# Linear attention and an eight-expert MoE on one Trainium2 core: token rows stored in 32 bits, split after the gather

## The chip, the core and the metric

The kernel runs on one core of one Trainium2 chip, in one launch. The metric is the device time of one execution in microseconds (us); lower is better. The times shown are the median of runs of the whole kernel, and the profile is of one execution.

Names of engines as in the profile: PE is TensorE's matmul, PEld its weight load, DVE is VectorE, ACT is ScalarE, POOL is GpSimd, SP is SyncE, which here only issues DMAs.

## The reference

Attention over 8 batches, 8 heads, 576 tokens and 64 columns per head with 128 random features, and then a mixture of 8 experts of which each token goes to one:

```python
q_s, k_s = q * scale, k * scale
def phi(x):
    h = einsum('bhsd,md->bhsm', x, omega) - sum(x * x, -1) / 2
    return exp(h - max(h, -1)) / sqrt(m)
kv = einsum('bhsm,bhsd->bhmd', phi(k_s), v);  z = sum(phi(k_s), axis=2)
attn = einsum('bhsm,bhmd->bhsd', phi(q_s), kv) / (einsum('bhsm,bhm->bhs', phi(q_s), z) + 1e-6)

x = attn as rows of tokens: [4608, 512]
logits = x @ w_gate;  e = argmax(logits);  gate = softmax(logits)[e]
eom = sigmoid(x @ w_output_gate)
out = gate * eom[e] * (relu(x @ w1[e]) @ w2[e])      # w1: 512 x 1024, w2: 1024 x 512
```

## The kernel before, in words

**Two halves, interleaved.** The attention is done in 32 units u, one for each head (8) and pair of batches (4 pairs j, 1152 tokens each, as 9 chunks of 128). When the eight units of a pair j are done, its tokens are routed. The experts' work is done in items of 128 rows that share an expert: list 0 has 8 items, list 1 has 8, list 2 has 9, and the last list has 24 places, of which 13 are used in the profiled execution, 38 items in all. Units of later pairs and items of earlier lists run at the same time; the last list's items run alone.

**Precision.** Matmul operands are split into two 16-bit halves, high (a cast) and low (the 32-bit value less the high half). The casts are on ACT or DVE, the subtractions mostly on POOL.

**A unit** (`unit`, line 453). After the matmuls `pn` with the values and with the gates' weights folded in, `divide` (719) scales the result on DVE into `xf(u)`: 9 chunks of 64 columns of the head's output and, beside them, 16 columns with this head's part of the logits. Then

- `hi_half` (742, instruction on line 743, DVE) casts the 64 columns to 16 bits into the tile `xs` of the head pair;
- `lo_half` (745, line 747, POOL) writes the low half beside it;
- `sum_up` (760, lines 763 to 767, POOL, the last one on DVE) adds the 16 logit columns to the sum `lga` over heads;
- `pair` (780, line 786, SP) writes `xs` of two heads to the DRAM tile `rows`, 512 bytes per token and head pair. A row of `rows` is 512 words of halves and 16 words of which the first is the token's scale.

**Routing** (`routing`, `listing`) is a chain of small DVE instructions that ends in the indices `gi` of the items' rows.

**An item** (`item`, 1369). `gather` (line 1446, POOL) fetches 128 rows by an indirect DMA into `gx(n)`, three buffers. Line 1458 (SP) turns the halves straight out of `gx(n)` by a transposing DMA into `xt(n)`, three buffers. `hidden` (line 1483, PE) multiplies them by w1, `relu` (1490, ACT) and `rest` (1494, DVE) make the two halves `hh` and `hl` of the hidden layer, `second` (1506 and 1514, PE) multiplies by w2, `scaled` (1567, ACT) scales by the word from `gx(n)` into `os(n)`, and `put` (1556, POOL) scatters the rows to the output. `gx(n)` comes free with `scaled(n)`, so gather n+3 waits for it. When the expert changes, new weights come by DMA (`bring`, lines 1402 and 1404, SP) and are split on ACT (`high`, 364) and DVE (`low`, 368).

**What sets the order.** Every step is given to `Plan` with its engine, an assumed cost, what it comes after and a rank. `Plan.order` (181) simulates the engines with these costs and writes one list; each engine executes its part of it strictly in that order. A step whose input is late holds up all that stands behind it on its engine. A gather is assumed to have landed 0.65 + 0.75 + 0.95 us after its instruction (at the earliest), and a change in any step's cost or inputs can move steps on all engines.

Of the kernel before, what the change touches and what calls it, by code (L numbers as in the profile page):

```python
# [21 lines left out]
P = 128  # L22
B, H, S, D, M = 8, 8, 576, 64, 128
NE, F = 8, 1024
N = B * S
DM = H * D
NSC = 4
NC = 9
NCV = 10
NP = H // 2  # L30
ROW = DM + 16
KEY = 64
KC = DM // P
GW = 2 * NE
W = 1 + D + GW
# [229 lines left out]
def attention_moe(ctx: ExitStack, tc: tile.TileContext, kqt, kqn, v, om, wg, w1, w2, cf, cm, ci, out):  # L265
    nc = tc.nc
# [34 lines left out]
    scales = const.tile([P, NC, ROW - DM], F32, name="scales")  # L301
# [108 lines left out]
    xf = buf("xf", 2, [NC, D + GW], F32)  # L410
    den = buf("den", 2, [NC], F32)
    xs = buf("xs", 2, [NC, P], F32)
# [40 lines left out]
    def unit(u):  # L453
        j, h = divmod(u, H)
# [262 lines left out]
        pr, o = u // 2, (u % 2) * D  # L717
# [13 lines left out]
        for c0, c1, pe, dve in ((0, 5, 0.6, 0.48), (5, NC, 0.42, 0.4)):  # L731
            plan.add(
                ("pn", u, c0), ("PE",), pe, lambda c0=c0, c1=c1: attend(c0, c1), after=[*turned_all, ("gl", u)], rank=R + 5,
                tiles=[("et", u), ("kvs", u)], bank=(cls, ("pn", u, c0), [c1 - c0, W]),
            )
            plan.chain(
                ("xf", u, c0), ("DVE",), (0.07, 0.1, dve), lambda c0=c0, c1=c1: divide(c0, c1), after=[("pn", u, c0)], rank=R + 5,
                tiles=[("xf", u), ("den", u)], frees=[("pn", u, c0)],
            )


        def hi_half():
            nc.vector.tensor_copy(xs(pr).bitcast(F16)[:, :, o : o + D], xf(u)[:, :, 0:D])  # L743

        def lo_half():
            x = xs(pr).bitcast(F16)
            nc.gpsimd.tensor_tensor(  # L747
                out=x[:, :, P + o : P + o + D], in0=xf(u)[:, :, 0:D], in1=x[:, :, o : o + D], op=ALU.subtract
            )

        plan.add(
            ("xh", u), ("DVE",), 0.37, hi_half, after=[("xf", u, 0), ("xf", u, 5)], rank=R + 6,
            tiles=[("xf", u), ("xs", pr)],
        )
        plan.add(
            ("xl", u), ("POOL",), 1.23, lo_half, after=[("xh", u)], rank=R + 6, tiles=[("xf", u), ("xs", pr)]
        )


        def sum_up():  # L760
# [12 lines left out]
            tiles=[("xf", u), ("lga", j)], bank=("e", ("rt", j), [512]) if end else None,  # L773
# [110 lines left out]
    def save_scales(j):  # L884
        nc.sync.dma_start(rows[j * NC * P : (j + 1) * NC * P, DM:].rearrange("(c p) r -> p c r", p=P), scales)
# [392 lines left out]

    gx = buf("gx", 3, [ROW], F32)
    xt = buf("xt", 3, [2 * KC, P], F16)  # L1280
# [88 lines left out]
    def item(n):  # L1369
# [75 lines left out]
        def gather():  # L1445
# [10 lines left out]
        )  # L1456
        add(
            ("xt", n), "SP", 0.63, lambda: nc.sync.dma_start_transpose(xt(n), gx(n)[:, 0:DM].bitcast(F16)),
            after=[("gx", n)], rank=-700.0 + n, tiles=[("xt", n), ("gx", n)], dma=0.9, turn=True,
# [105 lines left out]
        def scaled(w_):  # L1565
            d = DM * w_ // P
            nc.scalar.activation(os(n)[:, 0:d], banks["po", n][:, 0:d], AF.Copy, scale=gx(n)[:, DM : DM + 1])  # L1567
# [90 lines left out]
```

## Time and profile before

| | |
|---|---|
| runs | 667.91, 660.49, 665.92 us; median 665.92 |
| the profiled execution | 664.8 us, of which the span from the first to the last instruction is 663.0 |
| mean granted TensorE clock | 0.961 |
| busy: PE, DVE, ACT, POOL | 610.9, 425.7, 413.0, 340.5 us |
| DMA | 129.09 MB |
| first and last gather (line 1446) | 116.8 and 623.0 us |
| last unit's cast (line 743) | 465.4 us |

In order of time: 0 to 80 us are units in 32-bit matmuls, 80 to 130 the first routing, 130 to 440 units and items together, 440 to 500 the last routing beside items, and from 500 on items alone. Idle time of an engine costs something only where TensorE waits for it. In the views of waits a row reads: engine and line that waited, what it waited for, us in total, times, longest. In the timeline a row is start, duration, engine, line, operation, and in brackets idle time just before it.

### The profile page before, as it was taken

Reading aid. Unit: us, or ns where it says so; the run is one execution under the profiler, and the core shown is the slowest. Engines: PE = TensorE matmul, PEld = TensorE weight load, DVE = VectorE, ACT = ScalarE, POOL = GpSimd, SP = SyncE. Lnnn points to the kernel's source line nnn. Section 1 sums busy time; section 2 is a strip of 40 time slices with the busy share of each in tenths; the row PEclk is TensorE's granted clock in tenths of the full one; section 3 lists DMA queues with packets and bytes.
Section 4 is the critical chain, followed back from the end, with each engine's and each line's share of the span. In section 5 each row is a group of like instructions: output and inputs, shape, how many; then the busy total and the mean of one; then the engine's idle time right before and its main releaser. Section 6 shows DMA issues by size and latency. Waiting matters only on the chain. (4 is left out here: it accounts for less than half of the span.)

```text
span 663.0 us, 22360 instructions
## 1 busy us (share of the span) xinstructions
PE 610.9 (92%) x8732; PEld 479.8 (72%) x8732; DVE 425.7 (64%) x1277; ACT 413.0 (62%) x970; POOL 340.5 (51%) x235
## 2 busy tenths in 40 slices
PE   6999987799999899999788999999999899999972
PEld 6899976677777677777555777878677767676761
DVE  4899889876978897576587776753882611431160
ACT  5876887589989759898575588762611611521150
POOL 1342445569957958989376588965031312131110
PEclk9999977699999999999899999999999999999996
DMA  9544578997999979999999675877747647642730
GB/s 317 207 136 129 174 281 197 254 252 167 319 275 287 272 191 221 227 225 235 277 257 170 149 194 126 144 134 198 226 113 211 183 92 234 172 90 62 268 112 8
DMA packets 145895, 129.09 MB, mean 195 GB/s; under 512 B 104271, under 2 KB 127441, under 8 KB 144465
## 3 DMA queue, kind: packets, MB, share of 16 engines
q1 hardware_dynamic: 139760, 107.45, 64.0%
q0 software_dynamic: 5984, 19.72, 9.4%
q8 instruction: 85, 1.39, 0.9%
q14 instruction: 66, 0.53, 0.3%
HBM read 83.86 MB, written 19.30 MB: 156 GB/s over the span
## 5 line engine op out<-in xcount | busy, mean ns | idle before, releaser
L1483 PE MATMUL ph<-xt,w1h 128*128 128x128 f16 (+1 forms) x2432 | 205.2, 218 | 3.4 <-ACT os L1567 1.6
L1483 PE MATMUL ph<-xt,w1l 128*128 128x128 f16 (+1 forms) x1216 | 201.3, 218 | 0.0
L1483 PEld LDWEIGHTS <-w1h 128*128 128x128 f16 x2432 | 181.9, 98 | 10.8 <-issue 4.4
L543 ACT ACTIVATE ef<-pp,nb 128x128 f32<-128x128 f32 x576 | 162.8, 392 | 41.5 <-DVE nb L537 31.6
L1494 DVE SCALAR_TENSOR_TENSOR hl<-ph,hh 128x512 f16<-128x512 f32 (+1 forms) x76 | 50.6, 666 | 116.4 <-ACTq L1412 76.6
L566 POOL TENSOR_TENSOR es<-ef,es 128x1152 f16<-128x1152 f32 x44 | 104.9, 2391 | 35.6 <-ACT es L564 19.5
L524 DVE TENSOR_REDUCE pp<-pp 128x3 f32<-128x384 f32 x192 | 102.8, 557 | 28.2 <-PE pp L502 27.7
L1483 PEld LDWEIGHTS <-w1l 128*128 128x128 f16 x1216 | 118.5, 98 | 0.3 <-DVEq L1407 0.2
L1446 POOL DMA_INDIRECT gx<-rows,gi x38 | 40.8, 1074 | 140.5 <-ACT os L1567 100.6
L1514 PE MATMUL po<-w2h,hl 128*128 128x512 f16 x280 | 107.0, 382 | 2.4 <-DVEq L1412 1.5
L1514 PE MATMUL po<-w2h,hh 128*128 128x512 f16 x280 | 107.4, 384 | 0.0
L1514 PE MATMUL po<-w2l,hh 128*128 128x512 f16 x280 | 107.1, 383 | 0.0
L1490 ACT ACTIVATE hh<-ph 128x512 f16<-128x512 f32 (+1 forms) x76 | 44.3, 583 | 80.0 <-PE ph L1483 73.6
L1514 PEld LDWEIGHTS <-hh 128*128 128x128 f16 x560 | 51.9, 99 | 58.0 <-issue 3.7
L1567 ACT ACTIVATE os<-po,gx 128x512 f32<-128x512 f32 (+1 forms) x38 | 25.5, 670 | 72.9 <-PE po L1514 68.0
L436 POOL TENSOR_TENSOR xlo<-xt,xhi 128x1152 f16<-128x1152 f32 x24 | 57.2, 2382 | 13.2 <-ACT xhi L429 12.7
L713 PE MATMUL pn<-kvs,et 128*128 128x81 f16 (+1 forms) x960 | 48.2, 210 | 12.3 <-DMA et<-es 7.2
L713 PEld LDWEIGHTS <-et 128*128 128x128 f16 (+1 forms) x960 | 41.6, 105 | 21.2 <-DMA et<-es 7.9
L564 ACT CAST es<-ef 128x1152 f16<-128x1152 f32 x44 | 51.3, 1176 | 7.4 <-DMA et<-es 6.9
L1514 PEld LDWEIGHTS <-hl 128*128 128x128 f16 x280 | 27.6, 99 | 35.3 <-DVE hl L1494 1.3
L502 PE MATMUL pp<-omh,xhi 64*128 64x128 f16 x432 | 43.0, 223 | 5.0 <-DVE xf L726 2.7
L747 POOL TENSOR_TENSOR xs<-xf,xs 128x576 f16<-128x576 f32 x32 | 42.1, 1317 | 8.9 <-DVE xs L743 8.1
(183 smaller groups left out, 1052.8 us busy)
## 6 DMA issues: line engine op xcount, KB each, us to landing
r<-w SPq DMA_DIRECT2D x10, 2048.0 KB, 11.9
xt<-kqt SPq DMA_DIRECT2D x32, 576.0 KB, 4.7
xn<-kqn SPq DMA_DIRECT2D x24, 576.0 KB, 4.9
rawv<-v SPq DMA_DIRECT2D x32, 325.0 KB, 3.7
rows<-xs SPq DMA_DIRECT2D x16, 576.0 KB, 5.3
r<-w SPq DMA_DIRECT2D x8, 512.0 KB, 6.6
ef<-w SPq DMA_DIRECT2D x2, 512.0 KB, 4.4
et<-w SPq DMA_DIRECT2D x2, 512.0 KB
```

The lines of the kernel that those rows point to most:

```text
L436: lambda t0=t0, t1=t1: nc.gpsimd.tensor_tensor(out=xl(u)[:, t0:t1], in0=xt32(u)[:, t0:t1], in1=xh(u)[:, t0:t1], op=ALU.subtract),
L502: nc.tensor.matmul(banks["pp", 2 * u + i, g][:, c, :], x[r, t], w[r, :], start=(a == 0), stop=(a == len(ops) - 1))
L524: nc.vector.tensor_reduce(out=pp[:, 3, 0:3], in_=pp[:, 0:3, :], op=ALU.min, axis=AX.X)
L543: nc.scalar.activation(ef(n)[:, c, :], banks["pp", n, g][:, c % 3, :], AF.Exp, bias=nb(n)[:, c : c + 1], scale=-SK)
L564: nc.scalar.copy(es(slot_es(n))[:, 0], ef(n))
L566: nc.gpsimd.tensor_tensor(out=es(slot_es(n))[:, 1], in0=ef(n), in1=es(slot_es(n))[:, 0], op=ALU.subtract)
L713: nc.tensor.matmul(pn[lo:hi, c - c0, :], a[:, c, lo:hi], w[:, b, :], start=(i == 0), stop=(i == len(ops) - 1))
L747: nc.gpsimd.tensor_tensor(out=x[:, :, P + o : P + o + D], in0=xf(u)[:, :, 0:D], in1=x[:, :, o : o + D], op=ALU.subtract)
L1483: nc.tensor.matmul(ph[:, f4, 0:w_], w[qd][:, kk, fo : fo + P], xt(n)[:, x, 0:w_], start=(a == 0), stop=(a == 3 * KC - 1))
L1490: nc.scalar.activation(hh(n)[:, sl, 0:w_], banks["ph", n, g][:, :, 0:w_], AF.Relu)
L1494: nc.vector.scalar_tensor_tensor(out=hl(n)[:, sl, 0:w_], in0=banks["ph", n, g][:, :, 0:w_], scalar=0.0, in1=hh(n)[:, sl, 0:w_], op0=ALU.ma ...
L1514: nc.tensor.matmul(po, x(n)[:, f, :], w[f // 2][:, f % 2, :], start=(f == 0 and a == 0), stop=(f == FC - 1 and a == 2))
```

## The change

The 64 columns and the 16 logit columns stay together in 32 bits. `divide` writes straight into the pair's tile `xs`, now 9 x 2 x 80 words; `hi_half` and `lo_half` leave the unit, and `xf(u)` becomes a view of `xs`. The rows go to DRAM as they are, logits included: 320 bytes per token and head, so 640 in place of 512 per head pair, and a row of `rows` has 656 words in place of 528. Each item then splits its own 128 gathered rows: a cast on DVE (`row_half(0)`, step `xh`) and a subtraction on POOL (`row_half(1)`, step `xl`) from `gx(n)` into a new tile `xg(n)`, two buffers, and the transposing DMA reads `xg(n)`.

```diff
-ROW = DM + 16
+DW = D + GW
+XW = H * DW
+ROW = XW + 16
...
-    xf = buf("xf", 2, [NC, D + GW], F32)
     den = buf("den", 2, [NC], F32)
-    xs = buf("xs", 2, [NC, P], F32)
+    xs = buf("xs", 2, [NC, 2, DW], F32)
...
-        pr, o = u // 2, (u % 2) * D
+        pr = u // 2
+        xf = lambda u: xs(u // 2)[:, :, u % 2]
...
-                tiles=[("xf", u), ("den", u)], frees=[("pn", u, c0)],
-            )
-        def hi_half():
-            nc.vector.tensor_copy(xs(pr).bitcast(F16)[:, :, o : o + D], xf(u)[:, :, 0:D])
-        def lo_half():
-            x = xs(pr).bitcast(F16)
-            nc.gpsimd.tensor_tensor(
-                out=x[:, :, P + o : P + o + D], in0=xf(u)[:, :, 0:D], in1=x[:, :, o : o + D], op=ALU.subtract
-            )
-        plan.add(
-            ("xh", u), ("DVE",), 0.37, hi_half, after=[("xf", u, 0), ("xf", u, 5)], rank=R + 6,
-            tiles=[("xf", u), ("xs", pr)],
-        )
-        plan.add(
-            ("xl", u), ("POOL",), 1.23, lo_half, after=[("xh", u)], rank=R + 6, tiles=[("xf", u), ("xs", pr)]
-        )
+                tiles=[("xs", pr), ("den", u)], frees=[("pn", u, c0)],
+            )
...
-        both = [("xl", 2 * pr), ("xl", 2 * pr + 1)]
+        both = [("xf", 2 * pr + i, c0) for i in range(2) for c0 in (0, 5)]
...
-                rows[j * NC * P : (j + 1) * NC * P, hp * P : (hp + 1) * P].rearrange("(c p) r -> p c r", p=P), xs(pr)
+                rows[j * NC * P : (j + 1) * NC * P, hp * 2 * DW : (hp + 1) * 2 * DW].rearrange("(c p) r -> p c r", p=P),
+                xs(pr).rearrange("p c i d -> p c (i d)"),
             ),
-            after=both, rank=R + 0.5, tiles=[("xs", pr)], dma=1.64,
+            after=both, rank=R + 0.5, tiles=[("xs", pr)], dma=2.0,
...
+    xg = buf("xg", 2, [KC, 2, P], F16)
...
+        def row_half(which):
+            x = gx(n)[:, 0:XW].rearrange("p (k i d) -> p k i d", k=KC, i=2)[:, :, :, 0:D]
+            hi, lo = (xg(n)[:, :, i].rearrange("p k (i d) -> p k i d", i=2) for i in range(2))
+            if which == 0:
+                nc.vector.tensor_copy(hi, x)
+            else:
+                nc.gpsimd.tensor_tensor(out=lo, in0=x, in1=hi, op=ALU.subtract)
+        add(("xh", n), "DVE", 0.45, lambda: row_half(0), after=[("gx", n)], rank=-760.0 + n, tiles=[("gx", n), ("xg", n)])
+        add(("xl", n), "POOL", 1.2, lambda: row_half(1), after=[("xh", n)], rank=-805.0 + n, tiles=[("gx", n), ("xg", n)])
         add(
-            ("xt", n), "SP", 0.63, lambda: nc.sync.dma_start_transpose(xt(n), gx(n)[:, 0:DM].bitcast(F16)),
-            after=[("gx", n)], rank=-700.0 + n, tiles=[("xt", n), ("gx", n)], dma=0.9, turn=True,
+            ("xt", n), "SP", 0.63,
+            lambda: nc.sync.dma_start_transpose(xt(n), xg(n).rearrange("p k i d -> p (k i d)")),
+            after=[("xl", n)], rank=-700.0 + n, tiles=[("xt", n), ("xg", n)], dma=0.9, turn=True,
         )
```

The scale's column moves from word 512 to word 640 of the row (`save_scales`, `scaled`). The order is made anew by `Plan`. Three places of it follow; the line numbers of the changed kernel are other ones (its cast is on 1447, its subtraction on 1449, `rest` on 1491, the minima on 525, the gather on 1432).

VectorE near item 18, whose gather is `gx18`, before (`hl16` is item 16's low half, `pp_56` the projection of a unit):

```order
L726 TENSOR_TENSOR xf26_9041<-pn_26_5_9027,den26_9040 128x320
L659 SCALAR_TENSOR_TENSOR kvs27_9155<-kv_27_9044,kvs27_9155 128x2x65
L743 CAST xs13_9162<-xf26_9041 128x9x64
L1494 SCALAR_TENSOR_TENSOR hl16_9221<-ph_16_0_9101,hh16_9174 128x512
L524 TENSOR_REDUCE pp_56_2_9179<-pp_56_2_9179 128x3
L524 TENSOR_REDUCE pp_57_2_9180<-pp_57_2_9180 128x3
```

and in the changed kernel:

```order
L728 TENSOR_TENSOR xs13_9041<-pn_26_5_9013,den26_9040 128x4x80
L658 TENSOR_SCALAR kvs27_9142<-kv_27_9044 128x2x65
L660 SCALAR_TENSOR_TENSOR kvs27_9142<-kv_27_9044,kvs27_9142 128x2x65
L1447 CAST xg18_9175<-gx18_9080 128x4x128
L1491 SCALAR_TENSOR_TENSOR hl16_9203<-ph_16_0_9086,hh16_9153 128x512
L525 TENSOR_REDUCE pp_56_2_9155<-pp_56_2_9155 128x3
L525 TENSOR_REDUCE pp_57_2_9156<-pp_57_2_9156 128x3
```

The cast of the unit's own result is replaced by the cast of item 18's gathered rows; the residual of item 16 and the minima stand behind it as they stood behind the other.

GpSimd from gather 17 to gather 18 and on, before (`es` and `xlo` are the units' low halves, `vs` those of the values):

```order
L1446 DMA gx17_8695<-rows_69,gi2_8269 128x528
L1556 DMA out0<-os14_8634,oi1_5193 4608x512
L765 TENSOR_TENSOR lga3_8421<-lga3_8421,xf25_8637 128x144
L747 TENSOR_TENSOR xs12_8321<-xf25_8637,xs12_8321 128x9x64
L566 TENSOR_TENSOR es41_8578<-ef53_8441,es41_8578 128x1152
L436 TENSOR_TENSOR xlo29_8861<-xt3229_8045,xhi29_8849 128x1152
L587 TENSOR_TENSOR vs28_8766<-rawv28_8000,vs28_8766 128x650
...
L1446 DMA gx18_9164<-rows_69,gi2_8269 128x528
L1556 DMA out0<-os15_9082,oi1_5193 4608x512
L765 TENSOR_TENSOR lga3_8421<-lga3_8421,xf26_9041 128x144
L747 TENSOR_TENSOR xs13_9162<-xf26_9041,xs13_9162 128x9x64
L436 TENSOR_TENSOR xlo30_9287<-xt3230_8572,xhi30_9223 128x1152
```

and in the changed kernel:

```order
L1432 DMA gx17_8716<-rows_69,gi2_8306 128x656
L1553 DMA out0<-os14_8580,oi1_5138 4608x512
L749 TENSOR_TENSOR lga3_8217<-lga3_8217,xs12_8068 128x144
L588 TENSOR_TENSOR vs28_8718<-rawv28_7878,vs28_8718 128x650
L437 TENSOR_TENSOR xlo29_8838<-xt3229_8022,xhi29_8780 128x1152
L1449 TENSOR_TENSOR xg17_8847<-gx17_8716,xg17_8847 128x4x128
...
L1432 DMA gx18_9080<-rows_69,gi2_8306 128x656
L1553 DMA out0<-os15_9038,oi1_5138 4608x512
L749 TENSOR_TENSOR lga3_8217<-lga3_8217,xs13_9041 128x144
L588 TENSOR_TENSOR vs29_9145<-rawv29_8442,vs29_9145 128x650
L1449 TENSOR_TENSOR xg18_9175<-gx18_9080,xg18_9175 128x4x128
L437 TENSOR_TENSOR xlo30_9261<-xt3230_8477,xhi30_9199 128x1152
```

The subtraction that belonged to the unit is gone, and one that belongs to the gather just issued stands four or three instructions behind it.

VectorE near item 31 in the last list, in the changed kernel (the two forms of `hl29` are a block of at most 64 rows and a full one, of which one runs; `w1l` are splits of new weights, which run only if the expert changes; the branches between are left out):

```order
L1491 SCALAR_TENSOR_TENSOR hl29_13380<-ph_29_0_13243,hh29_13374 128x512
...
L370 SCALAR_TENSOR_TENSOR w1l0_94<-ef65_11338,w1h0_90 128x1024
...
L370 SCALAR_TENSOR_TENSOR w1l1_95<-ef66_11339,w1h1_91 128x1024
...
L1447 CAST xg31_13525<-gx31_13353 128x4x128
...
L1491 SCALAR_TENSOR_TENSOR hl29_13380<-ph_29_1_13384,hh29_13374 128x4x64
...
L1491 SCALAR_TENSOR_TENSOR hl29_13380<-ph_29_1_13384,hh29_13374 128x512
```

The cast of item 31's rows stands between the first and the second residual of item 29; before, nothing that waits for a gather stood on VectorE.

More of the change, by code (lines that the diff above doesn't have):

```diff
@@ L300, in attention_moe @@
     place = const.tile([P, NSC * NC, P], F16, name="place")
-    scales = const.tile([P, NC, ROW - DM], F32, name="scales")
+    scales = const.tile([P, NC, ROW - XW], F32, name="scales")
     nc.vector.memset(scales, 0.0)
@@ L772, in unit @@
             after=[("xf", u, 0), ("xf", u, 5)] + ([("lga", u - 1)] if h else []), rank=RANK_ROUTE + 80.0 * j if end else R + 5.5,
-            tiles=[("xf", u), ("lga", j)], bank=("e", ("rt", j), [512]) if end else None,
+            tiles=[("xs", pr), ("lga", j)], bank=("e", ("rt", j), [512]) if end else None,
         )
@@ L884, in save_scales @@
     def save_scales(j):
-        nc.sync.dma_start(rows[j * NC * P : (j + 1) * NC * P, DM:].rearrange("(c p) r -> p c r", p=P), scales)
+        nc.sync.dma_start(rows[j * NC * P : (j + 1) * NC * P, XW:].rearrange("(c p) r -> p c r", p=P), scales)
     def counts(j):
@@ L1566, in scaled @@
             d = DM * w_ // P
-            nc.scalar.activation(os(n)[:, 0:d], banks["po", n][:, 0:d], AF.Copy, scale=gx(n)[:, DM : DM + 1])
+            nc.scalar.activation(os(n)[:, 0:d], banks["po", n][:, 0:d], AF.Copy, scale=gx(n)[:, XW : XW + 1])
         add(
```

## The prediction

> **What bounds the kernel now.** I read the page's first part, then the stretches of the span, then who waits for whom, and last the gathers one by one in order of time.
>
> ```profile
> PE 610.9 (92%) x8732; PEld 479.8 (72%) x8732; DVE 425.7 (64%) x1277; ACT 413.0 (62%) x970; POOL 340.5 (51%) x235
> ...
> core 0: us, PE busy (x) PEld busy (x) DVE busy (x) ACT busy (x) POOL busy (x), PEclk, DMA share, GB/s
> ...
> 20.00:80.00 60.00, 59.27 (x815) 53.85 (x815) 53.62 (x149) 47.48 (x151) 26.23 (x19) 1.00 0.46 143
> 80.00:130.00 50.00, 39.28 (x512) 34.21 (x508) 42.98 (x179) 35.78 (x102) 23.50 (x17) 0.73 0.90 251
> 130.00:300.00 170.00, 165.71 (x2635) 129.07 (x2630) 133.52 (x426) 144.43 (x337) 134.43 (x87) 0.99 0.96 243
> 300.00:440.00 140.00, 130.14 (x2064) 99.75 (x2063) 100.79 (x329) 103.23 (x245) 103.37 (x67) 0.98 0.82 185
> ...
> 500.00:640.00 140.00, 134.88 (x1658) 98.62 (x1656) 40.52 (x52) 43.83 (x61) 28.90 (x26) 1.00 0.57 162
> ```
>
> TensorE is the bound nearly everywhere: 59 of 60 us, then 296 of 310 us from 130 to 440, then 135 of 140. Only from 80 to 130, where units are routed for the first time, is it idle for long; VectorE is busy 43 of those 50 us, and TensorE's granted clock there is 0.73. So an edit away from TensorE gains only what TensorE waits for, and loses only what makes it wait. From 130 to 440 VectorE is idle for 310 − 133.5 − 100.8 = 76 us and GpSimd for 310 − 134.4 − 103.4 = 72 us. What TensorE waited for there (waits of PE, 125 to 445):
>
> ```profile
> PE pn L713 <- DMA et<-es: 7.2, 2, 4.1
> PE pn L713 <- DVE kvs L700: 1.8, 1, 1.8
> ```
>
> No row of that view names the casts and subtractions that the change takes away.
>
> **Removed from the units.**
>
> ```profile
> L743 DVE CAST xs<-xf 128x576 f16<-128x576 f32 x32 | 29.6, 926 | 0.2
> L747 POOL TENSOR_TENSOR xs<-xf,xs 128x576 f16<-128x576 f32 x32 | 42.1, 1317 | 8.9 <-DVE xs L743 8.1 <-DVE nb L530 0.4 <-DMA xt<-kqt 0.4
> ...
> L743 DVE CAST xs<-xf x32: 479/599/2610, 26.3 to 465.4; 128x576 f16<-128x576 f32 x32
> ...
> 80.00:130.00 50.00, 2.07 (x4) 0.73 0.90 251
> 130.00:300.00 170.00, 10.50 (x11) 0.99 0.96 243
> 300.00:440.00 140.00, 8.22 (x9) 0.98 0.82 185
> ```
>
> 32 casts of 926 ns (29.6 us of VectorE) and 32 subtractions of 1317 ns (42.1 us of GpSimd) go. The last three rows are line 743 alone: 4 casts (2.07 us) in the stretch where VectorE is the bound, 20 (18.7 us) from 130 to 440. There the 20 subtractions are 20 x 1.317 = 26.3 us.
>
> **Added per item.** 38 gathers ran, so 38 casts and 38 subtractions come back, of 512 columns in place of 576. Scaled by 512/576 they are 926 -> 823 ns and 1317 -> 1171 ns: 31.3 and 44.5 us. The totals hardly change; what changes is where they stand. From 130 to 440 run 18 gathers (items 3 to 20), so VectorE gets 14.8 us for 18.7, GpSimd 21.1 for 26.3. That relief lies in idle time, and I give it 2 us, mostly for the 16 us of these instructions that no longer stand between a unit and its next transpose. Bounds: 0, and −9 if all of the 7.2 + 1.8 us of the two waits above went.
>
> The cast's spread, 479 to 2610 ns, is a wait inside the instruction. The Trainium skill (SBUF — State Buffer, Who interferes with whom) says that a cast that uses two ports and a GpSimd instruction exclude each other for a whole instruction, whichever began first. The spread agrees with that rule, and it speaks against adding casts where GpSimd is busy. By it 38 casts cost between 38 x 0.43 = 16 us (all alone, 479 ns scaled) and the 31 us above, and the sum would move by a small part of 15 us; I keep the mean.
>
> **The new wait.** This is the term that decides. Before, the only instruction that waits for a gather to land is the transpose on SP:
>
> ```profile
> SPq L1458 <- DMA gx<-rows,gi: 168.6, 33, 11.0
> ...
> gx<-rows,gi POOLq DMA_INDIRECT x38, 5.2
> xt<-gx SPq DMA_TRANSPOSE x38, 3.9
> ```
>
> A gather takes 5.2 us (median) and SP stood 168.6/33 = 5.1 us before each of 33 transposes, at no visible cost, as SP computes nothing. Now VectorE's cast waits for the landing, and behind it on VectorE, in program order, stand the item's residuals (L1494) and the units' minima (L524); GpSimd's subtraction waits for the cast, in front of the units' subtractions. The order shown above puts the cast of item 18 just ahead of item 16's first residual, that of item 31 ahead of item 29's second. Four places, each with the gather, the transpose that started as soon as it had landed, and the first VectorE instruction that would now stand behind the cast (items 4, 11, 18 and 31):
>
> ```profile
> 167.92 0.99 POOL L1446 DMA_INDIRECT gx<-rows,gi  x1
> 173.68 1.25 SPq L1458 DMA_TRANSPOSE xt<-gx  x1
> 170.22 1.02 DVE L524 TENSOR_REDUCE pp<-pp 128x3 f32<-128x384 f32 x2
> ...
> 279.18 0.99 POOL L1446 DMA_INDIRECT gx<-rows,gi  x1
> 284.79 1.24 SPq L1458 DMA_TRANSPOSE xt<-gx  x1
> 282.27 0.69 DVE L1494 SCALAR_TENSOR_TENSOR hl<-ph,hh 128x512 f16<-128x512 f32 x1 [2.18 <-ACT hh L1490]
> ...
> 401.50 1.00 POOL L1446 DMA_INDIRECT gx<-rows,gi  x1
> 407.35 1.24 SPq L1458 DMA_TRANSPOSE xt<-gx  x1
> 403.37 0.69 DVE L1494 SCALAR_TENSOR_TENSOR hl<-ph,hh 128x512 f16<-128x512 f32 x1 [1.67 <-ACT hh L1490]
> 408.05 0.38 PE L1514 MATMUL po<-w2h,hl 128*128 128x512 f16 x1
> ...
> 557.84 0.97 POOL L1446 DMA_INDIRECT gx<-rows,gi  x1 [8.24 <-ACT os L1567]
> 566.95 1.27 SPq L1458 DMA_TRANSPOSE xt<-gx  x1
> 562.82 0.69 DVE L1494 SCALAR_TENSOR_TENSOR hl<-ph,hh 128x512 f16<-128x512 f32 x1 [1.94 <-ACTq L1412]
> 564.11 0.38 PE L1514 MATMUL po<-w2h,hl 128*128 128x512 f16 x1 [1.53 <-DVEq L1412]
> ```
>
> With 0.7 us for handoff and an undisturbed cast, VectorE's next work moves by 173.7 + 0.7 − 170.2 = 4.2, 3.2, 4.7 and 4.8 us. These are bad cases: elsewhere the order leaves more work between gather and cast, so the bounds for the 18 items are 0 and 18 x 4.0 (mean of the first three) = 73 us. I take the middle, 2 us each, 36 us, which fits in VectorE's 76 idle us. How much reaches TensorE I read from item 18: its residual would end at 407.35 + 0.7 + 0.7 = 408.75, and the matmul that needs it ran at 408.05, so 0.7 of 4.7 us, about one sixth. 36/6 = **6 us** (bounds 0 and 36, or 73 with the larger wait, which would not fit the idle time). In the last stage TensorE has no units to fill with: at item 31 the matmul follows its residual at once, so the whole 4.8 us shows, **5 us** (bounds 0, if that gather lands sooner, and 10, if a second one meets a weight load).
>
> **From 80 to 130** VectorE loses 2.07 us of casts and gets three (items 0 to 2), 3 x 0.82 = 2.5 us, plus a short wait for the first two gathers: **+1 us** (bounds −2, if the casts take 479 ns and don't wait, and +4).
>
> **The item's chain** from landing to transpose grows by 0.2 + 0.8 + 0.2 + 1.2 = 2.4 us. The item with the least slack is the last:
>
> ```profile
> 633.16 1.28 SPq L1458 DMA_TRANSPOSE xt<-gx  x1
> ...
> 639.58 0.23 PE L1483 MATMUL ph<-xt,w1h 128*128 128x64 f16 x2
> ```
>
> 6.4 us from the transpose's start to its first use, less 3.9 to its landing, leaves 2.5: covered, just. Three buffers of gathered and of turned rows hide it for the others; without that cover each list's first item would cost 2.4 us, 10 us over the four lists.
>
> **DMA.** Rows and gathers carry 16 x 144 KB and 38 x 64 KB more, 4.9 MB in round numbers.
>
> ```profile
> DMA packets 145895, 129.09 MB, mean 195 GB/s; under 512 B 104271, under 2 KB 127441, under 8 KB 144465
> ```
>
> That is 3.8% of the bytes. From 130 to 300, where the DMA share is 0.96, it would be 170 x 0.038 = 6 us if DMA set the pace; TensorE does, at 166 of 170, so I count 0 (bounds 0 and 6). The pair's rows wait for the units' own divisions now and no longer for GpSimd, but the first gather hung on the list of rows, not on the rows: 0.
>
> **Sum**, on the profiled execution's 664.8 us: −2 + 6 + 5 + 1 = +10, so 674.8. The median of the three runs shown is 665.9, 1.1 above the profiled one; I forecast **675 us**, its own range 669 to 682.
>
> **The rivals.** (a) Hidden: VectorE's stalls vanish in its 24% of idle time and the 5 us of item 31 doesn't recur, because the weight load and the gather no longer meet. For it: one sixth is drawn from one place, and SP's 168 us cost nothing. Against it: at item 31 TensorE had waited 1.53 us already. 664.8 + 1 − 2 + 1 = 665 us. (b) Faster: GpSimd's queue is what holds back the units' transposes; with 26.3 us of subtractions replaced by 21.1, and none between a unit's division and its row write, the waits for et (7.2) and kvs (1.8) go and the 80 to 130 stretch keeps 2 us: 664.8 − 11 = 654 us. It decides if the new subtractions find their gather landed and cast, that is, if GpSimd has more than 5.2 + 1 us of work between the two. The rows below are the kinds that stand there. For item 18 it is the first, second and fourth, 1.0 + 0.5 + 1.5 = 3 us, which speaks against this rival; for item 17 it is all four, 5.4 us.
>
> ```profile
> 402.80 1.01 POOL L1556 DMA_INDIRECT out<-os,oi  x1 [0.30 <-PE ph L1483]
> 403.81 0.53 POOL L765 TENSOR_TENSOR lga<-lga,xf 128x144 f32<-128x144 f32 x1
> 405.49 2.40 POOL L436 TENSOR_TENSOR xlo<-xt,xhi 128x1152 f16<-128x1152 f32 x1
> 407.82 1.45 POOL L587 TENSOR_TENSOR vs<-rawv,vs 128x650 f16<-128x650 f32 x1
> ```
> (c) Worse: half of the 36 us reaches TensorE, 18, plus 10 in the last stage, 1 and −2: 664.8 + 27 = 692 us. For it: the gaps from 80 to 130 went with a clock of 0.73, so gaps may cost more than their length; against it, 76 idle us to absorb the waits.
>
> **How the numbers follow.** Forecast 0.47, hidden 0.30, faster 0.17, worse 0.06. One per cent, 6.7 us, is about what a measurement of this kernel can tell from no change. Slower by over 1%: 0.43 of the forecast, 0.03 of hidden, all of worse, 0.52. Within 1%: 0.04 + 0.27 + 0.02 = 0.33. Faster by over 1%: 0.15. The range reaches down to the middle of (b) and up to the start of (c): 655 to 687, which leaves out about 0.06 above and 0.09 below.
>
> **What would show it.** Right: among VectorE's waits a row for the new cast on the gather's DMA, about 30 to 50 us in all; GpSimd's new subtraction waiting for that cast; TensorE gaps after items' residuals (L1494's successor), one of some 5 us between 555 and 575; SP's wait for gathers gone and its wait for GpSimd in its place. Wrong: VectorE's wait for gathers under 15 us, or TensorE's idle time from 130 to 440 under 12 us (it is 14 now), or the last stage unchanged at 135 of 140.

## The result, and the profile after

The changed kernel takes 699.78 us (median of 4 runs, 698.57 to 702.17), the kernel before 666.08 beside it (4 runs, 660.49 to 667.91): a ratio of 1.0525, 95% interval 1.0457 to 1.0594. It is slower by some 34 us; the forecast was 675 us and the range ended at 687. (Where a ratio below is not the quotient of the two medians, it leaves out runs in a disturbed state.)

The profiled execution of the changed kernel has a span of 698.4 us against 663.0. Its page and its stretches, in the columns of those shown of before:

```profile
span 698.4 us, 22391 instructions
...
PE 617.3 (88%) x8732; PEld 476.4 (68%) x8732; DVE 421.9 (60%) x1283; ACT 412.7 (59%) x970; POOL 347.5 (50%) x241
...
DMA packets 145893, 133.93 MB, mean 192 GB/s; under 512 B 104270, under 2 KB 127440, under 8 KB 144464
```
```profile
20.00:80.00 60.00, 58.54 (x796) 52.91 (x794) 48.97 (x141) 45.85 (x149) 18.62 (x13) 1.00 0.47 150
80.00:130.00 50.00, 36.30 (x508) 31.76 (x504) 41.91 (x172) 35.82 (x98) 20.63 (x15) 0.80 0.89 244
130.00:300.00 170.00, 156.41 (x2425) 118.59 (x2426) 120.52 (x394) 131.39 (x308) 120.65 (x79) 0.97 0.98 238
300.00:440.00 140.00, 124.13 (x1872) 90.89 (x1871) 91.89 (x310) 98.49 (x229) 95.26 (x62) 0.98 0.84 196
500.00:640.00 140.00, 131.48 (x1591) 95.57 (x1589) 62.27 (x120) 42.23 (x60) 46.46 (x38) 1.00 0.56 147
```

VectorE is busy 421.9 us against 425.7, ScalarE 412.7 against 413.0, GpSimd 347.5 against 340.5: little more to do anywhere. TensorE ran the same 8732 matmuls, busy 6.4 us longer, and idle for 698.4 − 617.3 = 81.1 us against 52.1. So 29 of the 35.4 us are TensorE waiting. More than half of that lies in the attention stage: from 130 to 440 it is idle 13.6 + 15.9 = 29.5 us against 14.2. The other engines are less busy there too, which fits a wait that is handed from one to the next; these rows alone do not show it.

The start of an item's scaled output (line 1564) shows when the delay arises:

| item | before, us | after, us | later by |
|---|---|---|---|
| 0 | 149.9 | 150.9 | 1.0 |
| 6 | 245.9 | 257.3 | 11.4 |
| 12 | 346.9 | 364.1 | 17.2 |
| 18 | 446.3 | 470.9 | 24.6 |
| 24 | 516.6 | 546.3 | 29.7 |
| 30 | 580.8 | 614.9 | 34.1 |
| 37 | 649.9 | 684.6 | 34.7 |

Up to the end of attention 25 to 30 us are lost: 10 between items 0 and 6, then 5 to 7 for every six items. In the last lists, where only items run, 5 more come. (The places of the items among the units differ between the two orders, so the rows of the attention stage are good to some us only.) Then the waits by engine, of the changed kernel (waiter, what released it, total, times, longest):

```profile
POOL xg L1449 <- DVE xg L1447: 82.8, 26, 7.6
...
DVE xg L1447 <- DMA gx<-rows,gi: 42.1, 16, 6.7
...
DVE xg L1447 <- issue: 14.3, 4, 7.6
```
```profile
SPq L1455 <- POOL xg L1449: 126.7, 27, 11.9
```
```profile
L1449 POOL TENSOR_TENSOR xg<-gx,xg 128x512 f16<-128x512 f32 x38 | 47.5, 1250 | 100.1 <-DVE xg L1447 82.8 <-DVEq L1398 9.0 <-DVE pp L534 4.5
...
L1447 DVE CAST xg<-gx 128x512 f16<-128x512 f32 x38 | 19.4, 511 | 59.3 <-DMA gx<-rows,gi 42.1 <-issue 14.3 <-DVEq L1398 2.3
```

This is the chain that the prediction described: SP no longer waits for the landing (168.6 us before) but for GpSimd, GpSimd for the cast, and VectorE for the gather's DMA, 42.1 us as the profile names it. The four waits put down to "issue" belong to it too: in each of them the cast starts 0.1 us after its gather has landed. The longest of the four is this. The gather of item 13 was issued at 326.4; the tile's own view of that stretch gives its landing, then come VectorE, TensorE and SP there:

```profile
L1432 POOL DMA_INDIRECT gx<-rows,gi x1: 989/989/989, 326.4 to 326.4; - x1
...
DMA to landing us min/median/max: 13.5/13.5/13.5
```
```profile
340.00 0.43 DVE L1447 CAST xg<-gx 128x512 f16<-128x512 f32 x1 [7.56 <-issue]
340.35 1.02 DVE L525 TENSOR_REDUCE pp<-pp 128x3 f32<-128x384 f32 x2
341.28 0.68 DVE L1491 SCALAR_TENSOR_TENSOR hl<-ph,hh 128x512 f16<-128x512 f32 x1
```
```profile
338.30 0.38 PE L1511 MATMUL po<-w2h,hh 128*128 128x512 f16 x1 [1.89 <-issue]
...
342.02 0.39 PE L1511 MATMUL po<-w2h,hl 128*128 128x512 f16 x1 [2.48 <-DVE hl L1491]
```
```profile
332.77 0.39 SPq L770 DMA_DIRECT2D rows<-xs  x1
341.69 4.34 SPq L1455 DMA_TRANSPOSE xt<-xg  x1
```

326.4 + 13.5 = 339.9: the gather lands, and at 340.0 the cast runs, after VectorE has stood for 7.56 us. Behind it stand two minima of a unit and the residual of an earlier item; TensorE waits 2.48 us for that residual, right after another gap of 1.89. A pair's rows were sent to DRAM while this gather was in flight; of all 38 gathers the median landing is 5.4 us. So in this place some 2.5 of 7.6 us reach TensorE, a third, and more if the gap before it belongs to it.

What TensorE waits for overall (waits of PE, 125 to 445, where before had et 7.2 and kvs 1.8 at the head):

```profile
PE po L1511 <- DVE hl L1491: 5.1, 4, 2.5
PE kv L678 <- DVE kvs L660: 3.6, 3, 1.6
PE pp L503 <- ACT ef L544: 3.3, 4, 1.3
PE ph L1480 <- issue: 2.0, 6, 0.5
PE pn L714 <- DMA et<-es: 1.9, 2, 1.6
```

The residuals head the list, as said. But most of the lost time is in short gaps behind steps of the units (kvs, ef), and these the cast's wait need not have caused. The experiments had to tell it apart: the wait of VectorE for the landing (**theory 1**), or the new order of all the other instructions (**theory 2**), or bytes.

### The profile page after: what moved, and what is told of

Its sections match the earlier page's. It is cut to its first block, busy times and chain, and to the rows that moved or that the text cites. A ratio compares the mean times of both kernels' runs of the same rounds, so it can differ in the third digit from the quotient of the medians.

```text
span 698.4 us, 22391 instructions
## 1 busy us (share of the span) xinstructions
PE 617.3 (88%) x8732; PEld 476.4 (68%) x8732; DVE 421.9 (60%) x1283; ACT 412.7 (59%) x970; POOL 347.5 (50%) x241
## 3 DMA queue, kind: packets, MB, share of 16 engines
q0 software_dynamic: 5984, 22.21, 10.3%
## 5 line engine op out<-in xcount | busy, mean ns | idle before, releaser
L1480 PEld LDWEIGHTS <-w1h 128*128 128x128 f16 x2432 | 181.7, 98 | 17.2 <-issue 7.7
L544 ACT ACTIVATE ef<-pp,nb 128x128 f32<-128x128 f32 x576 | 162.9, 392 | 50.9 <-DVE nb L538 35.4
L1511 PE MATMUL po<-w2h,hl 128*128 128x512 f16 x280 | 108.8, 389 | 7.2 <-DVE hl L1491 5.5
L1511 PE MATMUL po<-w2h,hh 128*128 128x512 f16 x280 | 108.9, 389 | 3.6 <-issue 1.9
L1449 POOL TENSOR_TENSOR xg<-gx,xg 128x512 f16<-128x512 f32 x38 | 47.5, 1250 | 100.1 <-DVE xg L1447 82.8
L1447 DVE CAST xg<-gx 128x512 f16<-128x512 f32 x38 | 19.4, 511 | 59.3 <-DMA gx<-rows,gi 42.1
L714 PEld LDWEIGHTS <-et 128*128 128x128 f16 (+1 forms) x960 | 41.2, 104 | 15.2 <-issue 4.7
```

The costliest lines, as they stand in the source:

```text
L544: nc.scalar.activation(ef(n)[:, c, :], banks["pp", n, g][:, c % 3, :], AF.Exp, bias=nb(n)[:, c : c + 1], scale=-SK)
L714: nc.tensor.matmul(pn[lo:hi, c - c0, :], a[:, c, lo:hi], w[:, b, :], start=(i == 0), stop=(i == len(ops) - 1))
L1449: nc.gpsimd.tensor_tensor(out=lo, in0=x, in1=hi, op=ALU.subtract)
L1480: nc.tensor.matmul(ph[:, f4, 0:w_], w[qd][:, kk, fo : fo + P], xt(n)[:, x, 0:w_], start=(a == 0), stop=(a == 3 * KC - 1))
L1511: nc.tensor.matmul(po, x(n)[:, f, :], w[f // 2][:, f % 2, :], start=(f == 0 and a == 0), stop=(f == FC - 1 and a == 2))
```

## The experiments

Ratios are against the kernel before, run beside each on the same chip.

**Bytes alone.** The kernel before with rows of 656 words; otherwise its own order.

```diff
-ROW = DM + 16
+PW = P + 2 * 16
+XW = NP * PW
+ROW = XW + 16
```

Its items read the first 512 words with the padding among them, so its output is not the reference's.

> The kernel before, with its splits where they were, but rows of 656 words and a pair's write of 640 bytes per token, the added 128 bytes being zeros (two buffers are cleared once at the start; order of the steps as before). It moves the change's bytes and nothing else. If the 3.8% of extra DMA bytes were a large part of the 34 us: 680 us or more. If waits of VectorE and GpSimd are the cause (my theory): 666, within 4 us of before.

663.87 us against 661.91, ratio 1.0039 (1.0000 to 1.0079). In that order the 4.9 MB cost at most some 5 us, most likely 2 to 3. They are not the main cause.

**The cast later, and earlier,** in the planner's order: a lead of −3 us or of +2 us on the cast's dependence on the gather.

```diff
-        add(("xh", n), "DVE", 0.45, ..., tiles=[("gx", n), ("xg", n)])
+        add(("xh", n), "DVE", 0.45, ..., tiles=[("gx", n), ("xg", n)], lead={("gx", n): -3.0})
```

> The changed kernel, with one number of the plan different: each item's cast is planned 3 us later after its gather (6.6 us or more after the gather's start in place of 3.6), so that more work stands ahead of it on VectorE and of the subtraction on GpSimd. The same instructions, another order. In-order waits for the landing as the cause: most of VectorE's 42 + 14 us of waits for gathers and half of GpSimd's 83 us go, and the time falls to 675 to 685. If the mere loss of the old order is the cause, or the longer chain of an item: no fall, 697 to 710.

> The changed kernel with each item's cast planned 2 us earlier after its gather (1.6 us or more after the gather's start in place of 3.6), so that it stands further ahead on VectorE and waits longer for the same landing. If VectorE's waits set the loss: they grow by up to 2 us for each of 38 items, and the time rises to 710 to 730. If the order as such costs: about 700, or less.

Later: 687.37, ratio 1.0290 (1.0166 to 1.0413), with four executions spread from 677.61 to 689.16. Earlier: 707.45, ratio 1.0684 (1.0637 to 1.0732). The casts' groups, later and then earlier:

```profile
L1447 DVE CAST xg<-gx 128x512 f16<-128x512 f32 x38 | 29.1, 766 | 16.0 <-DVEq L1398 10.8 <-DMA gx<-rows,gi 3.3 <-DVE ctl L1059 0.7
```
```profile
L1447 DVE CAST xg<-gx 128x512 f16<-128x512 f32 x38 | 19.8, 522 | 133.7 <-DMA gx<-rows,gi 99.0 <-issue 22.4 <-DMA et<-es 6.5
```

VectorE stands 16.0, 59.3 and 133.7 us before the casts at ratios of 1.029, 1.0525 and 1.068. The direction is theory 1's. But with little wait left 2.9% remain (the execution with the 16.0 us was the longest of the four), and 74 us more of waiting cost only 11 us: VectorE's wait is not the whole. Of the three totals 2.8, 35.0 and 51.1 us belong to items 3 to 20, and 13.0, 19.8 and 70.6 to items 24 to 37, so most of the 74 us were added after the units had ended.

**Both splits on GpSimd, or both on VectorE** (there the subtraction becomes `nc.vector.tensor_tensor`, with a plan of 0.65 on VectorE).

```diff
-                nc.vector.tensor_copy(hi, x)
+                nc.gpsimd.tensor_copy(hi, x)
...
-        add(("xh", n), "DVE", 0.45, ..., rank=-760.0 + n, ...)
+        add(("xh", n), "POOL", 1.0, ..., rank=-806.0 + n, ...)
```

> The changed kernel with the item's cast on GpSimd too, so that nothing on VectorE waits for a gather; GpSimd waits for the landing and has 38 casts more. If VectorE's waits are what costs: 670 to 682. If GpSimd's waits are what costs, or its busy time: 700 or more.

> The changed kernel with the item's subtraction on VectorE too, so that nothing on GpSimd waits for a gather; VectorE has 38 subtractions more. If GpSimd's 83 us of waits in front of the units' subtractions are what costs: 670 to 682. If VectorE's waits are what costs: 700 or more. If each costs a part, both this run and the one before come out between.

> Both splits on GpSimd, and planned 3 us later after the gather for items 0 to 20; the rest as in the run with both on GpSimd. If what remained there over the kernel before (1.2%) is GpSimd's 57 us of waits for gathers: 660 to 666. If it is GpSimd's extra busy time or the order: 668 to 674.

GpSimd: 670.53, ratio 1.0116 (1.0039 to 1.0194); GpSimd with a lead of −3 us for the cast of the first 21 items: 668.57 against 662.73 (medians of all runs, ten of them from 658.74 to 672.37), ratio 1.0022 (0.9980 to 1.0063); VectorE: 719.77, ratio 1.0888 (1.0803 to 1.0972). On GpSimd the wait for the landing is as long as it was on VectorE:

```profile
POOL xg L1447 <- DMA gx<-rows,gi: 56.8, 28, 6.3
```

The two kernels with both splits there lose little, although GpSimd is busy 369.5 us in the first: it seems to matter which engine's queue is held. But the planner writes a new order for each of these kernels, so they don't yet tell theory 1 from theory 2.

**No wait for the landing, same order.** In the next kernels every instruction but the split's stands in the changed kernel's order. First the cast, then both halves, read a fixed tile in place of the rows (with both, the items' output is not the reference's).

```diff
-                nc.vector.tensor_copy(hi, x)
+                nc.vector.tensor_copy(hi, fixed)
```

> The changed kernel, instruction for instruction in the same order, but VectorE's cast reads one constant tile (0.37 everywhere, cleared once at the start) in place of the gathered rows, so it needn't wait for the gather; GpSimd's subtraction still does. It leaves out the true high halves. If VectorE's wait for the landing is what costs: 668 to 682. If the new order as such, or the later transposes, cost: 695 to 703, as the changed kernel.

> As the run before, and GpSimd's subtraction reads the constant tile too, so that neither engine, nor the transpose, waits for the gather (only the last scaling does). It leaves out both true halves. Order and instructions are still those of the changed kernel. If GpSimd's waits cost something beside VectorE's: 5 to 12 us below the run before; if VectorE's are all: within 4 us of it. What is left above the kernel before is the price of the order and of the casts' and subtractions' place.

689.29, ratio 1.0422 (1.0364 to 1.0481), and 684.53, ratio 1.0290 (1.0231 to 1.0350; one of its four executions took 1512.7 us). That is not 665, so theory 1 as it stood falls. Nor are these runs clean: the wait turned up inside the cast. The casts with both halves fixed, then the worst of them beside GpSimd:

```profile
L1449 DVE CAST xg<-fixed x38: 409/428/4034, 121.0 to 650.0; 128x512 f16<-128x512 f32 x38
```
```profile
335.09 1.46 POOL L590 TENSOR_TENSOR vs<-rawv,vs 128x650 f16<-128x650 f32 x1
...
335.13 4.03 DVE L1449 CAST xg<-fixed 128x512 f16<-128x512 f32 x1
...
336.48 2.39 POOL L569 TENSOR_TENSOR es<-ef,es 128x1152 f16<-128x1152 f32 x1
```

The median is 428 ns, but this cast began 0.04 us after a GpSimd instruction, ran on through that one and the next (which ended at 338.87) and itself ended at 339.16. With the wait, the cast starts when the gather lands and GpSimd mostly stands idle behind it; without the wait it meets GpSimd at work. Hence the next four.

**No cast at all, and a two-input addition in its place.** Same order again. The first two leave the cast out: the high half is a constant in two buffers that are filled once, and GpSimd subtracts it from a fixed tile (no wait for the landing) or from the gathered rows (GpSimd waits). The other two keep VectorE's instruction as an addition, of zeros to the rows, or of a fixed tile to itself.

```diff
-                nc.vector.tensor_copy(hi, x)
+                pass
...
+    kept = [sb.tile([P, KC, 2, P], F16, tag=f"xg_{i}", name=f"xg{i}", bufs=1) for i in range(2)]
+        nc.gpsimd.memset(kept[i], 0.37)
```

> Left out: the cast of the gathered rows; the high half is a constant in two buffers filled once, and GpSimd subtracts it from a fixed tile, so item outputs are not the reference's. Every other instruction stands in the changed kernel's order. Theory 1 (VectorE held at the cast, by the wait or by GpSimd's work beside it, is what costs): without the cast nothing holds it, 660 to 672 us, VectorE's row for xg gone and TensorE's gaps near the 39 us of before. Theory 2 (the new order of the other engines' instructions costs most): 680 to 690, as in the run with both reads on the fixed tile.

> Left out: the cast alone; the high half is a constant, GpSimd subtracts it from the gathered rows, so it waits for the landing and VectorE does not. Theory 1 (VectorE's hold): 660 to 675, with GpSimd's wait for the landing 50 to 130 us and TensorE not minding. Theory 2 (order): 680 to 690. Theory 3 (GpSimd's own new wait is what reaches TensorE, by way of its halves of keys and its bank steps): 685 to 700, far above the run without that wait.

> The whole computation; the cast is an addition of a tile of zeros (two inputs), same order, same waits. If the landing's wait is what costs (theory 1a): 695 to 710, as the changed kernel or a few us above for the longer instruction. If the lengthening of a cast beside GpSimd's work is what costs (theory 1b): 675 to 690, because the two-input form should not be lengthened.

> Left out: the rows of both halves; VectorE adds a fixed tile to itself for the high half and GpSimd subtracts from that fixed tile, so neither waits for the landing and the item outputs are not the reference's; the order is the changed kernel's. Theory 1 (VectorE's hold): the additions take 0.5 to 0.8 us each with no long ones, 662 to 675. Theory 2 (order): 680 to 690, no lower than the 684.5 of the run with the cast of the fixed tile.

No cast, no wait: 687.72 against 667.07, ratio **1.0315** (1.0246 to 1.0384). No cast, GpSimd waits: 693.16, ratio 1.0374 (1.0297 to 1.0451). Addition of zeros: 706.64, ratio 1.0613 (1.0532 to 1.0694). Addition of the fixed tile: 697.11, ratio 1.0374 (1.0274 to 1.0474). The page of the first, and its subtractions:

```profile
span 684.9 us, 22349 instructions
...
PE 612.4 (89%) x8732; PEld 477.0 (70%) x8732; DVE 406.8 (59%) x1245; ACT 413.3 (60%) x970; POOL 344.8 (50%) x244
```
```profile
L1456 POOL TENSOR_TENSOR xg<-fixed,xg 128x512 f16<-128x512 f32 x38 | 45.0, 1186 | 0.1
```

Neither VectorE nor GpSimd is held by the split (0.1 us of idle time before 38 subtractions), VectorE has 15 us less to do than in the changed kernel, and still 3.15% are lost. So in this order the hold is worth 1.0525 − 1.0315 = 0.021, 14 us (the two intervals give some 6 either way), and 0.0315, 21 us, is something else. The hold, so measured, is VectorE's wait, its cast's work, and what of the wait GpSimd and the transposition take over; against the kernel in which GpSimd still waits, VectorE's part is 1.0525 − 1.0374 = 0.015, 10 us. Whether GpSimd's own wait costs the 0.6% between is within the intervals. Item by item, the profiled execution without cast and waits is 14.5, 13.3, 15.2, 16.4, 21.3 and 21.5 us later than the kernel before at items 6, 12, 18, 24, 30 and 37. Most of its loss arises before item 6, and the last 5 us arise behind item 24, as in the changed kernel. The addition was no remedy: it has the full wait, and a longer instruction.

**The order alone.** The kernel before, with its own instructions, in orders that the planner writes when one number is changed: its cost of a pair's rows DMA (as in the change), two steps per item that issue nothing in the split's place, and its cost of a hand-off between engines.

```diff
-            after=both, rank=R + 0.5, tiles=[("xs", pr)], dma=1.64,
+            after=both, rank=R + 0.5, tiles=[("xs", pr)], dma=2.0,
```
```diff
+        add(("ih", n), "DVE", 0.45, lambda: None, after=[("gx", n)], ...)
+        add(("il", n), "POOL", 1.2, lambda: None, after=[("ih", n)], ...)
```
```diff
-    HANDOFF, DRAIN, ... = 0.19, 0.13, ...
+    HANDOFF, DRAIN, ... = 0.20, 0.13, ...
```

> The kernel before with one number of the planner changed, the one that the change also changes: its cost for a pair's rows DMA goes from 1.64 to 2.0. Every instruction is the kernel before's; only their order moves. Theory 1 (the steps that the change adds cost the time, through the places they take in the order): 662 to 672 us. Theory 2 (the time of the kernel before hangs on its exact order, and any other order that the planner writes leaves more of a unit's short chain in front of TensorE): 672 to 690, with TensorE's gaps 45 to 60 us and waits such as kv behind kvs and pp behind ef above the kernel before's.

> The kernel before with two steps per item in the plan that issue nothing (VectorE 0.45, GpSimd 1.2) between the gather and the transposition; every instruction is the kernel before's, the order moves as a planner that reckons with the split moves it. Theory 1 (these steps' places): 675 to 690, above the run with the rows' cost alone. Theory 2 (any other order): 672 to 690, and no further from the kernel before than that run.

> The kernel before with the planner's cost of a hand-off between engines at 0.20 in place of 0.19, a number that says nothing of this change; every instruction is the kernel before's. Theory 1: 662 to 670. Theory 2 (any other order): 670 to 690, that is a spread of orders as wide as most of the change's loss.

Against 662.42 for the kernel before: 665.14, ratio 1.0031 (0.9990 to 1.0073); 660.54, ratio 0.9905 (0.9856 to 0.9955); and 677.23 with three runs of four at 677 to 679 and one at 665, so no ratio is given. Theory 2 in its strong form, that any other order costs 2 or 3%, falls: one cost nothing, one has the lowest median of the study, and only the third may have lost some 2%. The places of the added steps cost nothing by themselves either (the empty steps). No run has the kernel before with all that the change alters in the plan at once.

**The changed kernel in another order,** hand-off at 0.20; then the same order without cast and waits; then both splits on GpSimd at 0.20. The second leaves out what the first kernel without a cast left out.

> The changed kernel with the planner's hand-off at 0.20 in place of 0.19: the same instructions in another order. Theory 1 (the cast's wait and the split's places cost the time in any order): 693 to 706. Theory 2 (a good part is the one order): anywhere in 675 to 705, and the difference to the changed kernel is a sample of that part.

> Left out: the cast of the gathered rows; the high half is a constant and GpSimd subtracts it from a fixed tile, so the items' outputs are not the reference's. Hand-off cost 0.20, so the order is that of the changed kernel at this hand-off cost, 1.0473 of the time before. If the 12 us between the changed kernel and the same order without cast and waits are the price of the hold, this loses about as much here: 680 to 685. If the high 687 of the first order was the chance of that order, this is 665 to 675.

> The whole computation, both splits on GpSimd, as in the run at 1.0116, with the planner's hand-off cost at 0.20: the same instructions in another order. If the split on GpSimd is cheap in any order: 662 to 675. If that run was a lucky order: 675 to 690.

694.77, ratio 1.0473 (1.0387 to 1.0559); 668.33 against 661.37, ratio 1.0115 (1.0036 to 1.0194); 668.35, ratio 1.0125 (1.0047 to 1.0204). The casts of the first, then the pages of the first and the second:

```profile
L1447 DVE CAST xg<-gx 128x512 f16<-128x512 f32 x38 | 23.4, 615 | 66.7 <-DMA gx<-rows,gi 49.0 <-issue 14.8 <-POOL vs L588 2.1
```
```profile
span 692.8 us, 22393 instructions
...
PE 618.4 (89%) x8732; PEld 482.9 (70%) x8732; DVE 427.0 (62%) x1283; ACT 413.4 (60%) x970; POOL 343.7 (50%) x241
```
```profile
span 662.6 us, 22366 instructions
...
PE 603.7 (91%) x8732; PEld 473.7 (71%) x8732; DVE 406.1 (61%) x1245; ACT 413.4 (62%) x970; POOL 342.2 (52%) x244
```

Here the hold is worth 1.0473 − 1.0115 = 0.036, 24 us (some 8 either way). And what remained without cast and waits, 21 us in the first order, is 8 us in this one, with the same instructions: 13 us, some 7 either way, belonged to that one order. Between the two profiled executions without cast (the second is the shortest of its four) lie 22.3 us: TensorE is idle 72.5 and 58.9 us in them, and busy 8.7 us longer in the first with the same 8732 matmuls; why it is busy longer, no run shows. So both theories hold in part:

| | order at 0.19 (the change) | order at 0.20 |
|---|---|---|
| whole change | 1.0525 | 1.0473 |
| without cast and waits | 1.0315 | 1.0115 |
| the hold (difference) | 0.021, 14 us | 0.036, 24 us |
| both splits on GpSimd | 1.0116 | 1.0125 |

The last row has the cast's work and the landing's wait, on another engine and in orders of its own. It ends where the kernel without cast ends in the second order. Of the kernels that do the whole computation with 32-bit rows, the best one, both splits on GpSimd with the cast planned later, is about as fast as the kernel before (1.0022, or 1.009 by the medians of all runs); none is faster.

## Why the prediction was wrong, by its own steps

- **TensorE is the bound, and only what makes it wait costs: right.** The engines' work is almost unchanged, TensorE's idle time grew by 29 of 35 us.
- **The cast waits for the landing, with VectorE's work behind it: right in mechanism.** Foretold was a wait of 30 to 50 us; it is 42.1 by name, 59.3 with the rest before the casts. GpSimd waits for the cast (82.8), SP for GpSimd (126.7). Item 18, whose cast the prediction read off, did what was written:

```profile
424.49 0.43 DVE L1447 CAST xg<-gx 128x512 f16<-128x512 f32 x1 [5.09 <-DMA gx<-rows,gi]
424.83 0.69 DVE L1491 SCALAR_TENSOR_TENSOR hl<-ph,hh 128x512 f16<-128x512 f32 x1
425.43 1.02 DVE L525 TENSOR_REDUCE pp<-pp 128x3 f32<-128x384 f32 x2
426.36 0.18 DVE L701 TENSOR_TENSOR kvs<-kv,kvs 128x32 f16<-128x32 f32 x1
```
```profile
426.60 0.23 PE L503 MATMUL pp<-omh,xhi 64*128 64x128 f16 x1 [0.88 <-DVE kvs L701]
```

Of the 5.09 us, 0.88 reach TensorE here, about the sixth that was foretold. They come by a unit's `kvs`, which stands behind the minima, and not by the residual.

- **The hold's price, 6 + 5 + 1 = 12 us: near the 14 us measured in this order, but by luck.** At hand-off 0.20 it is 24. The casts of items 3 to 20 (150 to 465 us) and of items 24 to 37 (520 to 700):

```profile
L1447 DVE CAST xg<-gx 128x512 f16<-128x512 f32 x18 | 10.3, 573 | 35.0 <-DMA gx<-rows,gi 20.7 <-issue 14.3
```
```profile
L1447 DVE CAST xg<-gx 128x512 f16<-128x512 f32 x14 | 6.0, 426 | 19.8 <-DMA gx<-rows,gi 16.9 <-DVEq L1398 2.3 <-POOL xg L1449 0.6
```

VectorE's lost time in the attention stage was foretold well: 36 us, against 35.0 of waits and 10.3 of casts. The share of it that reaches the end was not: the sixth was drawn from one place. In the profiles the changed kernel is behind the one without cast and waits by 13.2 us at item 24 and by 13.2 at item 37. So the hold's price fell in the attention stage, 13 us where 6 were put, 0.29 of 45.3; and the waits of the last stage show none, where 5 us were put. A part too small and a part too large cancelled. Over the whole kernel VectorE loses 59.3 + 19.4 = 78.7 us to waits and casts, and 14 reach the end, 0.18; at 0.20 it is 66.7 + 23.4 = 90.1 and 24, 0.27. The 76 idle us were no cushion.
- **The failed step is the sum.** The share above misses 7 us; a term that is not there misses more. Beside the hold the sum had −2 for the relief and nothing else, as if all other instructions kept their places: the order was read at two spots, items 18 and 31. The planner wrote a new order for the whole kernel, and the kernel without cast and waits shows +21 us in it (16 by item 24, 5 behind it), where the sum had −2. Thirteen of these, some 7 either way, go with the order alone (the same instructions at 0.20 lose 8). The other 8 are not settled: bytes (1.0000 to 1.0079 by themselves), the subtraction's latency in the item's chain, or the chance of that order too, since the kernels with GpSimd's splits spread from 1.002 to 1.0125. What in the order costs the 13 us was not isolated and stays open.
- **The relief, −2: not seen.** The waits for et fell from 7.2 to 1.9 us as rival (b) hoped, but kvs and ef took their place.
- **The cast's price: 823 ns foretold, 511 measured.** It mostly starts when GpSimd stands idle, waiting for it, so the mean of the units' casts, scaled, was too high a price. The rule of the Trainium skill (SBUF — State Buffer, Who interferes with whom) is that a cast that uses two ports and a GpSimd instruction exclude each other. The trace agrees with it where the wait is gone: 4.03 us beside GpSimd at work.
- **The last stage, +5: the number came, its mechanism did not.** Items 24 to 37 fall back 34.7 − 29.7 = 5.0 us. But without cast and waits they fall back as far: there they take 671.4 − 533.1 = 138.3 us, as in the changed kernel, and 133.3 in the kernel before (137.1 in the run with the bytes alone). So the cast's wait, 19.8 us here, is not what costs the 5 us; what does stays open, and that the number fits is luck. (With the cast planned earlier and 70.6 us of such waits they take 143 us, so a longer wait does cost something there.) The one gap of 5 us at item 31 did not come. The cast of item 31 again waits, 4.51 us, ahead of item 29's second residual, and 0.82 of it reach TensorE (the kernel before had a gap of 1.53 near this place, too):

```profile
599.00 0.43 DVE L1447 CAST xg<-gx 128x512 f16<-128x512 f32 x1 [4.51 <-DMA gx<-rows,gi]
599.34 0.68 DVE L1491 SCALAR_TENSOR_TENSOR hl<-ph,hh 128x512 f16<-128x512 f32 x1
```
```profile
596.07 0.39 PE L1511 MATMUL po<-w2h,hh 128*128 128x512 f16 x1 [1.53 <-ACTq L1398]
...
600.08 0.39 PE L1511 MATMUL po<-w2h,hl 128*128 128x512 f16 x1 [0.82 <-DVEq L1398]
```

- **Bytes, 0: right** within 0.8%. **80 to 130, +1: the number fits**, as item 0's scaled output starts 1.0 us later. But TensorE is idle 3.0 us longer in that stretch, and without the cast item 0 is as late (151.6), so the cause is not shown to be the cast.
- **The rivals.** (a) and (b) fell, the first because VectorE's idle time did not hide its waits, the second because the new subtractions stood 100.1 us waiting, 82.8 of them for the cast. (c) had the place and the sign, half of 36 us, and 692 as its time; it got a chance of 0.06. Of its reason, that gaps cost more than their length, little was seen: TensorE was busy 6.4 us longer beside 29 us more of idle time, and why was not tested. The range ended at the start of (c), and a new order of the other instructions had no price in it.

## What to carry to other kernels

A wait that costs nothing on an engine that only issues costs a share of its length on an engine that many short chains pass through: here VectorE's lost time came back at 0.18 and 0.27 of itself, all of it in the stage where such chains run, while kernels in which GpSimd takes over the same wait and the cast lose about 1%, in orders of their own. Where a planner rewrites the order, an edit's price is its own price plus a draw from the orders: here 13 us between two orders of the same instructions. So give the sum a term for it, and measure the edit in a second order before crediting the mechanism.

## What the runs showed of the hardware

- A cast on VectorE that begins beside GpSimd's work did not get in between two GpSimd instructions: the one above lasted through both, 4.03 us for 0.43. With both splits on VectorE one took 5.18 us, with three GpSimd instructions in that time.
- It isn't the cast alone. The addition with two inputs in SBUF has 674/692/2818 ns as shortest, median and longest; the longest:

```profile
156.53 2.40 POOL L569 TENSOR_TENSOR es<-ef,es 128x1152 f16<-128x1152 f32 x1
...
156.67 2.82 DVE L1449 TENSOR_TENSOR xg<-fixed 128x512 f16<-128x512 f32 x1
```

It ended at 159.49, 0.56 us after GpSimd's instruction; the expectation that two inputs would not be held was wrong. The Trainium skill (SBUF — State Buffer, Who interferes with whom) has that rule for an instruction with two SBUF inputs, and the trace agrees. A residual (SCALAR_TENSOR_TENSOR, one input in PSUM) was not held: at 334.36 of the run with both halves fixed it took 0.69 us, in the middle of a GpSimd instruction that ran from 332.75 to 335.16.
- An indirect gather's landing ranges from 3.4 to 13.5 us (median 5.4) in the changed kernel. An in-order engine that waits for it takes on that spread.
